# Sparse attention, then a Sinkhorn-gated mixture of experts: sums of x moved to other passes, stores and Sinkhorn rounds reordered

## The chip, the cores and the metric

The kernel runs on one core of a Trainium2 chip. The metric is the device time of one launch in microseconds, as a median of several runs. Lower is better.

## The reference

Attention with two sparse masks (a local band for half of the heads, a stride of 32 for the others), whose output is the input `x` of a mixture of eight experts. All experts run on all 2,304 tokens, and a softmax-like gate, made doubly stochastic by eight Sinkhorn rounds, weighs their outputs.

```python
scores = scale * np.matmul(q, k.transpose(0, 1, 3, 2))      # B, H, S, D = 4, 8, 576, 64
scores = np.where(masks[None, :, :, :], scores, -1000000000.0)
attn = softmax(scores)
x = (attn @ v).transpose(0, 2, 1, 3).reshape(2304, 512)

logits = x @ w_gate                                          # 512 x 8
P = np.exp(logits - logits.max())
for _ in range(8):
    P /= P.sum(1, keepdims=True) + 1e-09
    P /= P.sum(0, keepdims=True) + 1e-09
    P *= N / E
for e in range(E):                                           # 8 experts, 512 -> 1024 -> 512
    out += P[:, e:e + 1] * (np.maximum(x @ w1[e], 0.0) @ w2[e])
```

## The kernel before

Every float32 matrix product is made of three products of split operands (a high part and the rest). A split is one ScalarE copy (the high part) and one subtraction on GpSimd or VectorE (the rest).

**First stage, 36 slots.** Of 32 attention steps, eight run ahead of the loop over `slots` and one in each of its first 24 slots. A slot also takes 256 tokens through 128 hidden columns of expert 0, of whose columns the slots do the first half: `layer1` (twelve matmuls into a PSUM bank `ph`, then `rectify`, which writes `h` with ScalarE and VectorE) and `layer2` of the slot before (six matmuls into `y`). Attention writes `x`, split, into the on-chip tensor `reg`, in chunks of 512 tokens; `store_x` copies each finished chunk to memory (`xd`). At the end of a slot the list `work` runs what was put there by `at(slot, ...)`: pieces of the gate's generator `gating`, preparation of the next experts' first weights (`prep_w1`), and loads. `gating` yields 20 times: two for each of five stretches of tokens (logits, transposes), two for the start of the softmax, and one for each Sinkhorn round. A round is a chain on VectorE (sums of rows, a reciprocal, a multiplication, sums of columns), closed by one pair of matmuls `pc` that adds over partitions.

**Second stage, 90 steps `g`, three passes of 30.** A pass takes 768 tokens through all remaining 30 groups of 256 hidden columns. The first layer is a Strassen product: seven products `mul(...)` of six matmuls, on sums of weights and on sums of x (`s1` to `s4`), into the banks `ba`, `bb`, `bc`; `plus` adds them up on VectorE. In pass 1 the second layer is plain (`second`, 36 matmuls of 512 columns into `yg`, added to `acc` with the gate's weight on VectorE), and the weights' sums are formed, split and stored to memory as well (`prep_w1`, `prep_w2`). In passes 2 and 3 these are loaded again, and the second layer is a Strassen product too (`second_strassen`, 42 matmuls); there GpSimd makes most of the forms (`form_lo`, the sums in `finish_first`).

**Sums of x.** `build_s` makes `s1` to `s4` for one pass in units of 128 tokens and half of the inner columns: sums on GpSimd, a split, two stores to `sd`. For pass 1 (`p` = 0) it reads `reg`, in slots 8 to 22. For passes 2 and 3 the generator `later_sums` reads `x` back from `xd` with four loads for each unit; `next(later)` runs at the end of each step of pass 1 from `g` = 3 on, two for each of twelve units. There the rest of the split is GpSimd's.

**Order.** Instructions are issued in the order of the program, on each engine its own (the scheduling is manual), and almost all transfers are issued by SyncE, one queue: an issue that waits holds up all later ones. So the place of each call in the loops is the schedule.

Lines that matter: `store_x` L149; loads of q, k, v L202 and L204; `pc` L385; `y` stores L464; `build_s` L530, L539, L547, L550 (ScalarE copy), L553 (rest), L555 (stores); `load_w1g` L589; `prep_w1` L611 to L629 with `split` L177 and L178; `w2_sums` L643 to L650; `prep_w2` L674 to L682; matmuls of the first layer L692, of the second L721 (plain) and L822; `plus` L745; `relu_hi` and `relu_lo` L753 and L757; `m1` L914; the first scaling of `acc` by the gate L1111.

Of the kernel before, what the change touches and what calls it, by code (L numbers as in the profile page):

```python
# [55 lines left out]
def kernel(  # L56
# [9 lines left out]
    nc = tc.nc  # L66
# [358 lines left out]

    def layer1(u, c, ft):
        taken = begun[u, c[0], ft][1] if (u, c[0], ft) in begun else ()
        begin_layer1(u, c, ft, [dt for dt in range(NDT) if dt not in taken])
        rectify(u, c, ft)

    def rectify(u, c, ft):
        c0, n = c
        ph = begun.pop((u, c0, ft))[0]
        h = pools["h"].tile([P, 2, 4 * P], F32R, tag="h", name=f"h_{u}_{c0}_{ft}")
        nc.scalar.activation(h[:, 0, :n], ph[:, :n], AF.Relu)
        nc.vector.scalar_tensor_tensor(
            h[:, 1, :n], ph[:, :n], 0.0, h[:, 0, :n].bitcast(F32), op0=ALU.max, op1=ALU.subtract
        )
        hs[u, c0, ft] = h

    def layer2(u, c, ft, only=None):
# [8 lines left out]
        for i in range(nt) if only is None else only:  # L450
            y = ys[u, c0][i]
            for a, b, first in ((0, 0, True), (0, 1, False), (1, 0, False)):
                nc.tensor.matmul(  # L453
                    y, h[:, a, i * P : (i + 1) * P], w[:, b, :],
                    start=(ft == 0 and first), stop=(ft == FH - 1 and a == 1),
                )
            if ft == FH - 1:
                t = c0 // P + i
                if t < HEAD:
                    nc.scalar.activation(acc[:, t, :], y, AF.Copy)  # L460
                else:
                    o = acc[:, HEAD + t % STAGE, :]
                    nc.scalar.activation(o, y, AF.Copy)
                    nc.sync.dma_start(yd[:, t - HEAD, :], o)  # L464

# [53 lines left out]

    def build_s(p, k, th):  # L520

        st = pools["sb"].tile([P, 4, 2, P], F32, tag="sx", name=f"sx_{p}_{k}_{th}")
        x, s = st[:, :, 0, :], st[:, :, 1, :]
        t0 = 2 * TN * p + P * th
        if p:
            for i, (dh, t) in enumerate(((0, t0), (0, t0 + TN), (1, t0 + TN), (1, t0))):
                nc.sync.dma_start(st[:, i], xd[:, :, k + 2 * dh, t : t + P])  # L527
# [5 lines left out]
        else:  # L533
            for o, t in ((x[:, 0:4:3], t0), (x[:, 1:3], t0 + TN)):
                ci, c = divmod(t, CH)
                hi, lo = (
                    chunk(ci)[:, i, k : k + 3 : 2, c : c + P].bitcast(F32) for i in range(2)
                )
                nc.gpsimd.tensor_tensor(o, hi, lo, op=ALU.add)  # L539
        x11, x21, x22, x12 = (x[:, i, :] for i in range(4))  # L540
# [7 lines left out]
        yield  # L548
        so = pools["sb"].tile([P, 2, 4, P], F32R, tag="so", name=f"so_{p}_{k}_{th}")
        nc.scalar.activation(so[:, 0], s, AF.Copy)  # L550
        yield
        engine = nc.gpsimd if p else nc.vector
        engine.tensor_tensor(so[:, 1], s, so[:, 0].bitcast(F32), op=ALU.subtract)  # L553
        for j in range(2):
            nc.sync.dma_start(  # L555
                sd[:, p, :, j, k, P * th : P * (th + 1)], so[:, j].bitcast(F32)
            )
        yield
# [327 lines left out]
    def step(g):  # L886
# [16 lines left out]
        if new:  # L903
# [8 lines left out]
            part[g] = m1, u2, u3, bb, bc  # L912
            mul(g, "w11", "x11", ba, True)
            nc.scalar.activation(m1, ba[:, :TN], AF.Copy)  # L914
        if s:
# [6 lines left out]
        if new:  # L922
# [12 lines left out]
            if g >= NK:  # L935
                mul(g, "t3", "s3", bb, False)
                plus(u3, bb, m1)
                plus(u3, bc, u3)
            mul(g, "w21", "x12", ba, False)
            if strassen(g):  # L940
                r11 = r11s[g] = pools["early"].tile([P, TN], F32, tag="r11", name=f"r11_{g}")
# [8 lines left out]
            if not g:  # L950
                next(w2n, None)
                next(w2n, None)
                for x, only in rest:
                    layer2(*x, only)
            if g < NK:
                mul(g, "t3", "s3", bb, False)
# [132 lines left out]
    gat = gating()  # L1089
    for n, (k, th) in enumerate((k, th) for k in range(2) for th in range(3)):  # L1090
        w = build_s(0, k, th)
        for i in ((8, 9, 9), (10, 11, 11), (12, 15, 15), (16, 17, 17), (18, 19, 19), (19, 22, 22))[n]:
            at(i, next, w, None)
    w1_first = [prep_w1(g) for g in range(2)]
    for g, i, pieces_at in ((0, 9, (23, 24, 25, 26)), (1, 27, (29, 30, 31, 32))):
        at(i, load_w1g, g)
        for n in pieces_at:
            at(n, next, w1_first[g], None)
    for i, name in (
        (23, "x11"), (24, "s2"), (25, "s1"), (32, "x12"), (32, "s3"), (33, "x22"), (35, "s4"),  # L1100
    ):
        at(i, load_x, 0, name)
    at(27, load_w1g, 2)
    at(33, load_w2g, 0)
    for i, n in ((27, 1), (28, 2), (29, 1), (30, 1), (31, 1), (32, 1), (33, 1), (34, 1), (35, 1)):
        for _ in range(n):
            at(i, next, gat, None)
    ahead_of_second = {28: 2, 29: 1, 35: 1}

# [5 lines left out]
    slots = [(0, (c, 2 * P), ft) for c in range(0, NT, 2 * P) for ft in range(FH)]  # L1115
    prev = None
    for slot, (u, c, ft) in enumerate(slots):
# [4 lines left out]
        else:  # L1122
            layer1(u, c, ft)
        for _ in range(ahead_of_second.get(slot, 0)):
            next(gat, None)
        if slot == 1:
# [23 lines left out]
        for x in work.get(slot, ()):  # L1150
            x()
        prev = (u, c, ft)

    for x in w1_first:
        for _ in x:
            pass
    stacks["left"].close()
    stacks["sums"].close()
# [3 lines left out]
    pools["u"] = ctx.enter_context(tc.tile_pool(name="u", bufs=2, side="left"))  # L1162
    open_pools("left", ("rab", 1), ("sb", 1))

    def later_sums():
        for p in range(1, NPASS):
            for k in range(2):
                for th in range(3):
                    w = build_s(p, k, th)
                    next(w)  # L1170
                    yield
                    next(w)
                    yield
                    for _ in w:
                        pass

    later = later_sums()
    for g in range(NG + 1):
        if g == NK:
            open_pools("left", ("early", 2))  # L1180
        if g == NK + 1:
# [20 lines left out]
        p, n = divmod(g, NK)  # L1202
        if 0 < p < NPASS:
# [86 lines left out]
```

## Time and profile before

| | |
|---|---|
| median of three runs | 1582.55 us (1581.46 to 3079.31) |
| the profiled execution: its time, its span | 1586.01 us, 1584.2 us |
| busy: TensorE, its weight loads, VectorE, ScalarE, GpSimd | 98%, 92%, 83%, 35%, 66% of the span |
| moved by DMA | 433.63 MB, mean 274 GB/s |

The profile is of one execution. A row of the timeline is one instruction, or several alike in a row: start and duration in us from the start of the span, engine, line, what is written and read, its shape, how many, and in brackets how long the engine had been idle and what ended that. PE is TensorE, DVE VectorE, ACT ScalarE, POOL GpSimd, SPq the queue of SyncE. Matmuls overlap by some tenths of a microsecond, so that six in a row that start 1.04 us after the six before them may be shown with 1.20 us.

### The profile page before, as it was taken

What the parts mean: (1) busy time and instruction counts of PE and PEld (TensorE: products, weight loads), DVE (VectorE), ACT (ScalarE), POOL (GpSimd) and SP (SyncE); (2) the same over time, 40 slices, a digit from 0 to 9 for tenths busy, and PEclk for the clock granted to TensorE, in tenths of its full rate; (3) what the DMA queues carried; (4) which work ended last, traced back from release to release, by engine and by line L of the source; (5) the groups of instructions that cost most, each with busy time, mean ns of one, the idle gap of its engine ahead of it and who ended that gap; (6) DMA issues with size and microseconds to landing.
All of it is one profiled execution on the core that took longest, in us unless ns stands there. A gap on an engine that the chain in (4) does not pass through costs nothing.

```text
span 1584.2 us, 25846 instructions
## 1 busy us (share of the span) xinstructions
PE 1551.0 (98%) x9182; PEld 1459.8 (92%) x9182; DVE 1315.3 (83%) x2545; ACT 548.3 (35%) x1293; POOL 1050.0 (66%) x1033
## 2 busy tenths in 40 slices
PE   8999989999999999999999999999999999999999
PEld 6878879988888888899999999999999999999998
DVE  5656579999999999977888888888868888888887
ACT  6656234334434443333233222222143222222221
POOL 4335425776767667627787777778677778777774
PEclk9999999999999999999999999999999999999999
DMA  7466868898999989888676667667667667666662
GB/s 222 154 207 212 291 231 323 329 356 324 331 340 347 353 325 324 332 289 327 276 292 252 246 266 277 246 242 289 243 249 291 266 241 288 257 236 271 271 239 95
DMA packets 138225, 433.63 MB, mean 274 GB/s; under 512 B 10129, under 2 KB 82673, under 8 KB 123121
## 3 DMA queue, kind: packets, MB, share of 16 engines
q1 hardware_dynamic: 137952, 431.86, 72.0%
q8 instruction: 73, 1.20, 0.3%
q14 instruction: 56, 0.45, 0.1%
q10 hardware_dynamic: 144, 0.13, 0.0%
HBM read 287.20 MB, written 144.75 MB: 273 GB/s over the span
## 4 chain that ended last, share of the span: by engine, by line
PE 69%; DVE 12%; DMA 5%; POOL 5%; issue 3%; ACT 3%; SPq 3%; POOLq 0%; ACTq 0%; DVEq 0%
PE p L822 26%; PE bb L692 13%; PE ba L692 8%; PE bc L692 8%; PE yg L721 4%; DMA raws<-in_w 3%; DVE acc L728 3%; PE y L453 2%; PE ph L420 2%; POOL reg L178 2%; DVE u L745 2%; DVE w2t L682 2%; DVE w2b L682 2%; SPq L527 2%; DVE h L757 1%
## 5 line engine op out<-in xcount | busy, mean ns | idle before, releaser
L830 DVE TENSOR_TENSOR total<-p,total 128x384 f32<-128x384 f32 x770 | 400.7, 557 | 0.8 <-PE p L822 0.8
L692 PE MATMUL bb<-reg 128*128 128x384 f32 x1620 | 330.1, 338 | 10.6 <-DVE u L745 10.6
L692 PEld LDWEIGHTS bb<-reg 128*128 128x128 f32 x1620 | 285.2, 188 | 20.4 <-DVE u L745 17.9
L692 PE MATMUL ba<-reg 128*128 128x384 f32 x1080 | 217.6, 336 | 2.5 <-ACT m L914 2.2
L692 PE MATMUL bc<-reg 128*128 128x384 f32 x1080 | 217.2, 335 | 0.0
L803 ACT ACTIVATE a<-u 128x384 fp32r<-128x384 f32 x114 | 59.9, 525 | 387.5 <-DVE u L797 387.2
L692 PEld LDWEIGHTS ba<-reg 128*128 128x128 f32 x1080 | 190.5, 189 | 3.1 <-ACT m L914 2.5
L879 POOL TENSOR_TENSOR s1t<-m,u 128x384 f32<-128x384 f32 x57 | 57.9, 1016 | 202.0 <-DVE m L797 202.0
L692 PEld LDWEIGHTS bc<-reg 128*128 128x128 f32 x1080 | 189.4, 188 | 2.2 <-ACT h L753 2.2
L745 DVE TENSOR_TENSOR u<-bb,m 128x384 f32<-128x384 f32 x180 | 99.7, 554 | 110.4 <-PE bb L692 110.2
L728 DVE SCALAR_TENSOR_TENSOR acc<-yg,gate,acc 128x512 f32<-128x512 f32 x198 | 139.8, 742 | 9.7 <-PE yg L721 9.6
L721 PE MATMUL yg<-w2b,h 128*128 128x512 f32 x540 | 126.3, 392 | 0.0
L721 PE MATMUL yg<-w2t,h 128*128 128x512 f32 x540 | 125.5, 390 | 0.0
L822 PE MATMUL p<-s,w2b 128*128 128x384 f32 x696 | 125.3, 334 | 0.0
L721 PEld LDWEIGHTS yg<-w2b,h 128*128 128x128 f32 x540 | 101.9, 189 | 20.8
L822 PEld LDWEIGHTS p<-s,w2b 128*128 128x128 f32 x696 | 121.1, 188 | 0.0
L822 PE MATMUL p<-s,w2t 128*128 128x384 f32 x672 | 121.0, 334 | 0.0
L721 PEld LDWEIGHTS yg<-w2t,h 128*128 128x128 f32 x540 | 101.2, 188 | 20.5
L807 POOL TENSOR_TENSOR a<-u,a 128x384 fp32r<-128x384 f32 x114 | 117.2, 1028 | 0.0
L822 PEld LDWEIGHTS p<-s,w2t 128*128 128x128 f32 x672 | 116.9, 188 | 0.0
L745 DVE TENSOR_TENSOR u<-bc,u 128x384 f32<-128x384 f32 x180 | 99.6, 553 | 4.1 <-PE bc L692 1.0
L178 POOL TENSOR_TENSOR reg<-rt,reg 128x512 fp32r<-128x512 f32 x28 | 36.3, 1297 | 94.1 <-ACT reg L177 94.1
(147 smaller groups left out, 2862.3 us busy)
## 6 DMA issues: line engine op xcount, KB each, us to landing
reg<-wd SPq DMA_DIRECT2D x56, 1792.0 KB
wd<-reg SPq DMA_DIRECT2D x30, 1792.0 KB
w2b<-w2d SPq DMA_DIRECT2D x27, 1792.0 KB
w2t<-w2d SPq DMA_DIRECT2D x26, 1792.0 KB
w2d<-w2b SPq DMA_DIRECT2D x15, 2048.0 KB
w2d<-w2t SPq DMA_DIRECT2D x15, 2048.0 KB
raws<-in_w SPq DMA_DIRECT2D x68, 256.0 KB
sd<-so SPq DMA_DIRECT2D x36, 256.0 KB
```

Source lines behind the costliest of these rows:

```text
L178: nc.gpsimd.tensor_tensor(lo, src, hi.bitcast(F32), op=ALU.subtract)
L420: nc.tensor.matmul(ph[:, :n], w[:, i, dt, :], xv(x, dt, c0, n), start=(first and len(taken) == 1 and i + x == 0), stop=(len(taken) == NDT ...
L682: nc.vector.tensor_tensor(w[:, 1, : 4 * Q], src, w[:, 0, : 4 * Q].bitcast(F32), op=ALU.subtract)
L692: nc.tensor.matmul(out[:, :TN], w[:, i, k, :], xops[x][:, xi, k, :], start=(start and n == 0), stop=(n == 5), skip_group_check=True,)
L721: nc.tensor.matmul(y, hg[g, i // 3, f][:, a, o : o + P], w[:, b, f, :], start=(f == 0 and a + b == 0), stop=(f == 1 and a == 1),)
L728: nc.vector.scalar_tensor_tensor(acc[:, i, :], y, gate[:, t, e : e + 1], acc[:, i, :], op0=ALU.mult, op1=ALU.add)
L745: nc.vector.tensor_tensor(o, bank[:, :TN], s, op=ALU.add)
L803: nc.scalar.activation(t[:, 0], src, AF.Copy)
L807: nc.gpsimd.tensor_tensor(t[:, 1], src, t[:, 0].bitcast(F32), op=ALU.subtract)
L822: nc.tensor.matmul(y[:, :TN], w[:, b, wi, d, :], h[:, a, :], start=(a + b == 0), stop=(a == 1),)
L830: nc.vector.tensor_tensor(o, y[:, :TN], o, op=ALU.add)
L879: nc.gpsimd.tensor_tensor(s1, m1, u3, op=ALU.add)
```

## The change

- `build_s` takes a width and whether it reads `reg` (`direct`). The six units of pass 2 are built, as those of pass 1, from `reg` in the slots (12 units, first stage in slots 8 to 25). The units of pass 3 stay with `later_sums`, in halves of 64 tokens (12 units), and `next(later)` runs in steps 32 to 59, which is pass 2.
- Of a unit in the slots, the split's two halves run together one slot after the sums, and the two stores to `sd` one slot later still. Rows of `y` go through `outbox` and are stored at the end of the slot after the one that made them.
- `layer1` can run rounds of `gating` between its matmuls and `rectify`. They run there in slots 27 to 35; the last two come in step 0, after its first product and after its fourth.
- The first scaling of `acc` runs on GpSimd as six multiplications with a broadcast operand, in step 0 behind the rest of `layer2`; before, ScalarE ran it at the end of step 0.
- `prep_w1(0)` moves from slots 23 to 26 to slots 23, 26, 27, 28; the raw weights of `g` = 1 are loaded in slot 28 and not 27; `x11`, `s2`, `s1` are loaded in slots 28, 28, 29 and not 23, 24, 25.

```diff
-    def layer1(u, c, ft):
+    def layer1(u, c, ft, between=0):
         taken = begun[u, c[0], ft][1] if (u, c[0], ft) in begun else ()
         begin_layer1(u, c, ft, [dt for dt in range(NDT) if dt not in taken])
+        for _ in range(between):
+            next(gat)
         rectify(u, c, ft)
...
                     nc.scalar.activation(o, y, AF.Copy)
-                    nc.sync.dma_start(yd[:, t - HEAD, :], o)
+                    outbox.append((yd[:, t - HEAD, :], o))
...
-    def build_s(p, k, th):
+    def build_s(p, k, o, w, direct):
-        st = pools["sb"].tile([P, 4, 2, P], F32, tag="sx", name=f"sx_{p}_{k}_{th}")
+        st = pools["sb"].tile([P, 4, 2, w], F32, tag="sx", name=f"sx_{p}_{k}_{o}")
...
-        so = pools["sb"].tile([P, 2, 4, P], F32R, tag="so", name=f"so_{p}_{k}_{th}")
+        so = pools["sb"].tile([P, 2, 4, w], F32R, tag="so", name=f"so_{p}_{k}_{o}")
         nc.scalar.activation(so[:, 0], s, AF.Copy)
+        engine = nc.vector if direct else nc.gpsimd
+        engine.tensor_tensor(so[:, 1], s, so[:, 0].bitcast(F32), op=ALU.subtract)
         yield
-        engine = nc.gpsimd if p else nc.vector
-        engine.tensor_tensor(so[:, 1], s, so[:, 0].bitcast(F32), op=ALU.subtract)
         for j in range(2):
-            nc.sync.dma_start(
-                sd[:, p, :, j, k, P * th : P * (th + 1)], so[:, j].bitcast(F32)
-            )
+            nc.sync.dma_start(sd[:, p, :, j, k, o : o + w], so[:, j].bitcast(F32))
...
             mul(g, "w11", "x11", ba, True)
+            if not g:
+                next(gat)
             nc.scalar.activation(m1, ba[:, :TN], AF.Copy)
...
             mul(g, "w21", "x12", ba, False)
+            if not g:
+                assert next(gat, gat) is gat
...
                 for x, only in rest:
                     layer2(*x, only)
+                send_out()
+                for i in range(HEAD):
+                    nc.gpsimd.tensor_tensor(
+                        acc[:, i, :], acc[:, i, :], gate[:, i, 0:1].to_broadcast([P, D]),
+                        op=ALU.mult,
+                    )
...
-    for n, (k, th) in enumerate((k, th) for k in range(2) for th in range(3)):
-        w = build_s(0, k, th)
-        for i in ((8, 9, 9), (10, 11, 11), (12, 15, 15), (16, 17, 17), (18, 19, 19), (19, 22, 22))[n]:
-            at(i, next, w, None)
+    units = [(p, k, P * th) for p in range(2) for k in range(2) for th in range(3)]
+    for x, i in zip(units, (8, 9, 11, 12, 14, 15, 19, 20, 21, 22, 24, 25)):
+        w = build_s(*x, P, True)
+        for n in range(3):
+            at(i + n, next, w, None)
     w1_first = [prep_w1(g) for g in range(2)]
-    for g, i, pieces_at in ((0, 9, (23, 24, 25, 26)), (1, 27, (29, 30, 31, 32))):
+    for g, i, pieces_at in ((0, 9, (23, 26, 27, 28)), (1, 28, (29, 30, 31, 32))):
...
-        (23, "x11"), (24, "s2"), (25, "s1"), (32, "x12"), (32, "s3"), (33, "x22"), (35, "s4"),
+        (28, "x11"), (28, "s2"), (29, "s1"), (32, "x12"), (32, "s3"), (33, "x22"), (35, "s4"),
...
-    for i, n in ((27, 1), (28, 2), (29, 1), (30, 1), (31, 1), (32, 1), (33, 1), (34, 1), (35, 1)):
-        for _ in range(n):
-            at(i, next, gat, None)
-    ahead_of_second = {28: 2, 29: 1, 35: 1}
+    for i in (27, 27, 28):
+        at(i, next, gat, None)
+    ahead_of_second = {27: 1, 28: 1, 29: 2, **{i: 1 for i in range(30, 36)}}
...
+        send, keep = keep, []
+        for x in send:
+            nc.sync.dma_start(*x)
+        keep, outbox[:] = outbox[:], []
...
     def later_sums():
-        for p in range(1, NPASS):
-            for k in range(2):
-                for th in range(3):
-                    w = build_s(p, k, th)
+        for k in range(2):
+            for o in range(0, TN, P // 2):
+                w = build_s(2, k, o, P // 2, False)
...
-            if g == 0:
-                assert next(gat, gat) is gat
-                for i in range(HEAD):
-                    scale(0, i)
-            if g > 2:
-                next(later, None)
         elif g < NK + KEEP:
             for store in put_off[g - NK :: KEEP]:
                 store()
+        elif g < 2 * NK:
+            next(later, None)
```

## Rows read from the trace of the kernel before

**Rows 1.** Who waited for whom, TensorE, whole span: us, times, longest

```profile
PE bb L692 <- DVE u L745: 10.6, 23, 0.9
PE pc L385 <- DVE g L382: 6.2, 5, 2.5
PE ba L692 <- ACT m L914: 2.2, 1, 2.2
```

**Rows 2.** Windows, one step each: length, busy (instructions) by engine, PE clock, DMA share, GB/s

```profile
256.72:272.23 15.51, 15.51 (x80) 14.07 (x80) 15.21 (x21) 6.26 (x11) 8.98 (x8) 1.00 0.87 316
...
303.47:319.80 16.33, 16.01 (x79) 14.00 (x79) 15.15 (x20) 6.28 (x12) 12.66 (x14) 1.00 0.95 344
...
662.60:678.11 15.51, 15.51 (x80) 14.07 (x80) 13.83 (x21) 6.11 (x11) 4.90 (x4) 1.00 0.77 288
```

**Rows 3.** Timeline of VectorE, the same line without and with sums of x alongside

```profile
268.75 0.55 DVE L757 SCALAR_TENSOR_TENSOR h<-u,h 128x384 fp32r<-128x384 f32 x1
...
431.31 1.08 DVE L757 SCALAR_TENSOR_TENSOR h<-u,h 128x384 fp32r<-128x384 f32 x1
```

**Rows 4.** Timelines of SyncE's queue and of TensorE, 78 to 100 us

```profile
78.58 1.43 SPq L555 DMA_DIRECT2D sd<-so  x2
...
83.46 0.53 SPq L149 DMA_DIRECT2D xd<-reg  x1
84.09 0.96 SPq L202 DMA_DIRECT2D qk<-in_qkv  x1
...
95.36 0.56 PE L220 MATMUL sc<-qk 64*64 64x96 f32 x16 [1.77 <-DMA qk<-in_qkv]
...
97.67 3.23 PE L348 MATMUL pl<-reg,wgs 128*128 128x512 f32 x8
```

**Rows 5.** Window over the last rounds and steps 0 and 1, columns as Rows 2

```profile
181.00:226.00 45.00, 35.41 (x189) 31.58 (x188) 31.85 (x82) 17.07 (x32) 13.63 (x12) 0.93 0.58 212
```

**Rows 6.** Timeline of TensorE: the last rounds before step 0, and step 1

```profile
199.72 0.39 PE L385 MATMUL pc<-g,ones 128*128 128x8 f32 x2 [0.94 <-DVE g L382]
202.57 0.47 PE L385 MATMUL pc<-g,ones 128*128 128x8 f32 x2 [2.47 <-DVE g L382]
...
221.91 1.32 PE L692 MATMUL ba<-reg 128*128 128x384 f32 x6 [2.18 <-ACT m L914]
```

**Rows 7.** Timelines of ScalarE and GpSimd around the first scaling

```profile
216.88 3.79 ACT L1111 ACTIVATE acc<-acc,gate 128x512 f32<-128x512 f32 x6 [1.28 <-DVE gate L389]
...
222.46 1.30 POOL L178 TENSOR_TENSOR reg<-ra,reg 128x512 fp32r<-128x512 f32 x1 [29.33 <-ACT reg L177]
```

**Rows 8.** Groups of GpSimd's instructions by shape: count, busy us, mean ns, idle before

```profile
L547 POOL TENSOR_TENSOR sx<-sx 128x128 f32<-128x128 f32 x72 | 31.7, 462 | 2.8
...
L530 POOL TENSOR_TENSOR sx<-sx 128x256 f32<-128x256 f32 x24 | 21.6, 919 | 0.0
...
L539 POOL TENSOR_TENSOR sx<-reg 128x256 f32<-128x256 f32 x12 | 8.5, 731 | 0.0
```

**Rows 9.** Timeline of TensorE, layer2 of slots 3, 4 and 11, 12

```profile
43.73 1.66 PE L453 MATMUL y<-w2t,h 128*128 128x512 f32 x6
48.52 1.68 PE L453 MATMUL y<-w2t,h 128*128 128x512 f32 x6
...
84.68 1.66 PE L453 MATMUL y<-w2t,h 128*128 128x512 f32 x6
89.47 1.68 PE L453 MATMUL y<-w2t,h 128*128 128x512 f32 x6
```

**Rows 10.** Timeline of SyncE's queue, and a window, columns as Rows 2

```profile
180.74 8.76 SPq L464 DMA_DIRECT2D yd<-acc  x4
...
185.00:190.00 5.00, 3.72 (x23) 3.13 (x24) 4.27 (x11) 2.87 (x7) 3.87 (x4) 1.00 0.13 52
```

**Rows 11.** A step of pass 2: window, columns as Rows 2; timeline of GpSimd

```profile
940.00:954.57 14.57, 14.57 (x86) 14.57 (x85) 12.53 (x24) 3.84 (x8) 11.04 (x11) 1.00 0.64 253
...
966.79 1.02 POOL L879 TENSOR_TENSOR s1t<-m,u 128x384 f32<-128x384 f32 x1 [3.36 <-DVE m L797]
```

More of the change, by code (lines that the diff above doesn't have):

```diff
@@ L439, in rectify @@
         hs[u, c0, ft] = h
+    outbox = []
     def layer2(u, c, ft, only=None):
@@ L518 @@
     wraw, w2raw, w2s, hg, yg, part = {}, {}, {}, {}, {}, {}
-    def build_s(p, k, th):
-        st = pools["sb"].tile([P, 4, 2, P], F32, tag="sx", name=f"sx_{p}_{k}_{th}")
+    def build_s(p, k, o, w, direct):
+        st = pools["sb"].tile([P, 4, 2, w], F32, tag="sx", name=f"sx_{p}_{k}_{o}")
         x, s = st[:, :, 0, :], st[:, :, 1, :]
-        t0 = 2 * TN * p + P * th
-        if p:
+        t0 = 2 * TN * p + o
+        if direct:
+            for d, t in ((x[:, 0:4:3], t0), (x[:, 1:3], t0 + TN)):
+                ci, c = divmod(t, CH)
+                hi, lo = (
+                    chunk(ci)[:, i, k : k + 3 : 2, c : c + w].bitcast(F32) for i in range(2)
+                )
+                nc.gpsimd.tensor_tensor(d, hi, lo, op=ALU.add)
+        else:
             for i, (dh, t) in enumerate(((0, t0), (0, t0 + TN), (1, t0 + TN), (1, t0))):
-                nc.sync.dma_start(st[:, i], xd[:, :, k + 2 * dh, t : t + P])
+                nc.sync.dma_start(st[:, i], xd[:, :, k + 2 * dh, t : t + w])
             yield
@@ L532, in build_s @@
                 )
[L533 to L537, printed above, removed]
-                )
-                nc.gpsimd.tensor_tensor(o, hi, lo, op=ALU.add)
         x11, x21, x22, x12 = (x[:, i, :] for i in range(4))
@@ L548, in build_s @@
         yield
-        so = pools["sb"].tile([P, 2, 4, P], F32R, tag="so", name=f"so_{p}_{k}_{th}")
+        so = pools["sb"].tile([P, 2, 4, w], F32R, tag="so", name=f"so_{p}_{k}_{o}")
         nc.scalar.activation(so[:, 0], s, AF.Copy)
+        engine = nc.vector if direct else nc.gpsimd
+        engine.tensor_tensor(so[:, 1], s, so[:, 0].bitcast(F32), op=ALU.subtract)
         yield
-        engine = nc.gpsimd if p else nc.vector
-        engine.tensor_tensor(so[:, 1], s, so[:, 0].bitcast(F32), op=ALU.subtract)
         for j in range(2):
-            nc.sync.dma_start(
-                sd[:, p, :, j, k, P * th : P * (th + 1)], so[:, j].bitcast(F32)
-            )
+            nc.sync.dma_start(sd[:, p, :, j, k, o : o + w], so[:, j].bitcast(F32))
         yield
@@ L954, in step @@
                     layer2(*x, only)
+                send_out()
[3 more added lines that the diff above has]
+                        op=ALU.mult,
+                    )
             if g < NK:
@@ L1115 @@
     slots = [(0, (c, 2 * P), ft) for c in range(0, NT, 2 * P) for ft in range(FH)]
-    prev = None
+    prev, keep = None, []
     for slot, (u, c, ft) in enumerate(slots):
@@ L1122 @@
         else:
-            layer1(u, c, ft)
-        for _ in range(ahead_of_second.get(slot, 0)):
-            next(gat, None)
+            layer1(u, c, ft, ahead_of_second.get(slot, 0))
         if slot == 1:
@@ L1156, with send_out @@
             pass
+    def send_out():
+        for x in keep + outbox:
+            nc.sync.dma_start(*x)
     stacks["left"].close()
@@ L1162 @@
     pools["u"] = ctx.enter_context(tc.tile_pool(name="u", bufs=2, side="left"))
-    open_pools("left", ("rab", 1), ("sb", 1))
+    open_pools("left", ("rab", 1))
     def later_sums():
-        for p in range(1, NPASS):
-            for k in range(2):
-                for th in range(3):
-                    w = build_s(p, k, th)
[L1170 to L1175, printed above, removed]
+        for k in range(2):
+            for o in range(0, TN, P // 2):
+                w = build_s(2, k, o, P // 2, False)
+                next(w)
+                yield
+                next(w)
+                yield
+                for _ in w:
+                    pass
     later = later_sums()
@@ L1179 @@
         if g == NK:
-            open_pools("left", ("early", 2))
+            open_pools("left", ("early", 2), ("sb", 1))
         if g == NK + 1:
```

## Prediction

> **What bounds the kernel now.** I read the waits first. TensorE waits in three places that this change touches: for `plus` ahead of the last product of pass 1's steps, 10.6 us in 23 times; for Sinkhorn rounds, 6.2 us; once 2.2 us for ScalarE [rows 1]. Then the windows, one step each, because a mean over the span hides the stages. A step of pass 1 without sums of x lasts 15.51 us with TensorE busy all of it, one with them 16.33 [rows 2]. Of passes 2 and 3 a step is 14.57 us, TensorE without a gap [rows 11]: nothing is to be won there. Last the timelines of the two places before pass 1 where TensorE stood still: one late load of q and k at 95 us [rows 4], and the stretch 181 to 226 us, in which it was busy 35.4 of 45.0 us at a mean granted clock of 0.93, that is, partly at 1.2 in place of 2.4 GHz [rows 5].
>
> **Sums leave pass 1.** The reader is to see that the long steps have no more matmuls, but up to 12.7 us of GpSimd in place of 9.0, with VectorE at 15.2 of 15.5 already without them [rows 2]. The one slows the other: a subtraction that took 0.55 us takes 1.08 beside the sums [rows 3]. So `plus` comes late and TensorE waits. The long steps run from 303.47 to 662.60 us, 22 of them of 16.32 us; the two before them (272.23 to 303.47) are 0.1 longer each than 15.51 [rows 2]. 22 x 0.81 + 0.2 = 18.1 us. All of it goes if every step is like 256.72 to 272.23. But there VectorE has only 0.3 us of room, so TensorE may lose half of that 0.1 in each of the 24 steps, 1.2 in all. I take 17.5; bounds 16.3 and 18.1.
>
> **Sums for pass 2 in the slots.** A unit costs GpSimd two sums of 0.73 us and four of 0.46, 3.3 us [rows 8], as well as a copy and a subtraction. TensorE covers it: from slot 11 to slot 12, with a unit's sums at work, its `layer2` matmuls start 4.79 us apart, and 4.79 from slot 3 to slot 4, without one [rows 9]. GpSimd also has each slot's normalizing, so four units in a row fill it; what waits for that is the transposes one slot later. I take nothing. Without the cover, half of each sum of the six new units would show, 10 us; below nothing there is nothing to win, as these slots have no wait of this kind.
>
> **Stores a slot later.** At 78.58 us SyncE's queue stands before a unit's stores, which wait for the split; behind them are the store of a chunk of x (83.46) and the load of q and k (84.09) that TensorE waits 1.77 us for at 95.36 [rows 4]. Issued a slot later, these stores hold up nothing there, and chunk and load go out earlier; no row says by how much, and I take it to be more than the 1.77. The wait is followed by a lower clock: eight logits matmuls take 3.23 us [rows 4]. For that I take half of the loss over 181 to 226 us, where two waits over 2 us did the same: 0.07 x 45.0 = 3.15 us [rows 5], so 1.6. Together 3.4; bounds 0 (the chunk of x still lies ahead of the load) and 3.4.
>
> **Rounds and scaling, 181 to 226 us.** 9.6 us idle and 3.15 of clock, 12.7 in all [rows 5]. Term by term:
> - A round with nothing beside it makes TensorE wait 2.47 us [rows 6]; that was the seventh, at the end of slot 35. It now comes behind the first product of step 0 (84 matmuls are a step of 14.57 us [rows 11], so its six take 1.04), and 1.4 remain. The other waits for rounds, 6.2 - 2.47 = 3.7 us, come in three slots where GpSimd slows the chain, and once, 0.94, in slot 35 [rows 6]. The order within a slot changes nothing for the three, as a round still needs the round before; the fourth goes. So -1.1 and -0.9.
> - The last round moves ahead of VectorE's work on the second weights, and GpSimd's six scalings begin right then. A GpSimd operation of this size takes 1.30 us [rows 7], so 7.8 us in which four operations of VectorE, ahead of the `plus` that TensorE waits for (0.9 at 213.64, the longest of its kind [rows 1]), can be stretched by 0.53 each [rows 3]. Bounds: 0 and +2.1; the late chain adds to that, so I take +0.8.
> - ScalarE no longer holds 3.79 us of scaling ahead of the copy of `ba`: the 2.18 us wait goes [rows 6, 7], and 0.3 beside it. GpSimd has been idle for 29 us by then [rows 7], so its scalings delay nothing of its own. -2.5.
> - One of the two clock drops goes with the 2.18, -1.6; bounds 0 and -3.15.
>
> Sum -5.3; bounds -1 and -12.7.
>
> The Trainium skill, page "SBUF — State Buffer", section "Who interferes with whom", has GpSimd and a VectorE operation with two SBUF inputs exclude each other for a whole instruction. Here a stretch of 0.53 us stands beside GpSimd operations of 1.30, so less than a whole one [rows 3, 7]. By the rule the four operations could lose 1.30 each, an estimate of 5.2 in place of 0.8, and the sum below would be 4.4 us smaller.
>
> **Loads before step 0.** `x11`, `s2`, `s1` move from slots 23 to 25 into a busy stretch, and the raw weights of `g` = 1 now go behind the store of `g` = 0's. But between 185 and 190 us DMA is used at 0.13, as the queue stands 8.76 us before stores of `y`, which are put off now [rows 10]. That room takes most of it. I allow 1.0 us for late raw weights; bounds 0 and 4.
>
> **Sums for pass 3 in pass 2.** GpSimd is idle for 3.36 us of each step, just where `next(later)` puts the work [rows 11]. A half unit's sums: two of half of 0.92, four of 0.23 to 0.46 [rows 8], so 1.8 to 2.8 us every second step; the other steps get a subtraction and a copy. All within 3.36; DMA is at 0.64. I take nothing. Upper bound: 0.5 us in each of 24 steps, 12 us, if the first form of the next step comes that late and all slack is gone.
>
> **Sum.** -17.5 - 3.4 - 5.3 + 1.0 = -25.2. The profiled execution, 1586.0, would be 1560.8. It lies 3.5 over the median of the runs shown, so the median goes from 1582.55 to 1557.4 us, 1.6% faster.
>
> **Rivals.**
> 1. Everything before pass 1 goes right: 18.1 + 3.4 + 12.7 = 34.2 us, so 1548. For it: each of the waits has a part of the change aimed at it. Against it: rounds are a chain, and moving them ahead of `rectify` doesn't shorten it. Faster than 2% needs 31.7, so 10.2 of the 12.7.
> 2. VectorE becomes the bound of pass 1. It is busy 15.21 of 15.51 us without the sums [rows 2], and its operations change with how they meet GpSimd's. With one more of them stretched, 15.21 + 0.53 = 15.74 us, and 24 x 0.23 = 5.5 of the full 18.1 is lost, 4.9 of my 17.5: 1562.3. Against it: two steps without sums, one early and one late, run at 15.51 [rows 2].
> 3. The slots pay: six units at 1.0 us, and 4 for late loads in place of 1.0, so 9 less: 1566.5. For it: four units in a row fill GpSimd, and ScalarE and VectorE stand in order behind it. Against it: slots 11 and 12 [rows 9].
> 4. The load of q and k stays late: 1561; within the forecast's own range.
> 5. Slower than before: pass 2. If GpSimd's additions don't fit into its gap, its 11 us chain of forms [rows 11] starts late and the second layer's matmuls wait for it. The kernel is slower than before once that costs 25.2 / 24 = 1.05 us a step, and slower by 2% from (25.2 + 31.7) / 24 = 2.4 us. At 1.5 us: 1593. Against it: 2.8 is under 3.36 even at the dear end.
>
> **Chances.** About 2%, 31.7 us, is what a measurement of this kernel can tell from no change. The forecast with rival 4, from 1552 to 1561.5: 0.64. Rival 1: 0.11, nearly all of it under the 2% line. Rival 2: 0.11. Rival 3: 0.10. Rival 5: 0.04, of which 0.02 would be over 2% slower. Range 1548 to 1566: it takes in rivals 1 and 2 and most of 3. Faster 0.10, same 0.88, slower 0.02.
>
> **What would show it.** Right: step 256 to 272's length in all steps of pass 1 and no waits `bb` for `plus`; no wait for q and k after the warm-up; nothing over 2 us before `ba` in step 1, with one wait of some 1.4 before `pc` in step 0; 14.57 us steps in pass 2 with GpSimd's idle time ahead of the first form down to some 1 us. Wrong: a wait of transposes for GpSimd's normalizing in slots 20 to 26; ScalarE idle for raw weights for more than 3 us around slot 29; waits of TensorE for forms in pass 2, which would make even the sign doubtful.

## The result and the profile after

| | before | after |
|---|---|---|
| median of the runs, us | 1582.57 | 1568.91 |
| profiled execution, us | 1586.01 | 1568.56 |
| its span, us | 1584.2 | 1566.7 |

The ratio is 0.9917, 95% interval 0.9904 to 0.9931: 13.7 us gained, under 1%, where 25.2 were forecast. The time lies 2.9 us above the upper end of the range.

In the trace after, code lines are 2 to 4 higher: 694 for 692 (products), 747 for 745 (`plus`), 682 and 684 for 680 and 682 (second weights). First who waited for whom, TensorE, whole span (us in total, times, longest), the answer to [rows 1]:

```profile
PE y L457 <- ACT h L437: 6.0, 1, 6.0
PE bb L694 <- DVE u L747: 5.4, 1, 5.4
...
PE pc L385 <- DVE g L382: 1.3, 1, 1.3
```

The 23 waits for `plus` have become one. The five for rounds have become one, and the one for ScalarE is gone. In their place stand two long waits, one in the last slots and one between steps 0 and 1, before pass 1 runs evenly. The windows (length, busy and instructions by engine, clock, DMA share, GB/s) show two steps of pass 1, the answer to [rows 2], one step of pass 2, the answer to [rows 11], and the two stretches with the long waits:

```profile
256.87:272.37 15.50, 15.50 (x80) 14.06 (x79) 14.99 (x21) 6.27 (x11) 8.96 (x8) 1.00 0.87 320
303.51:319.01 15.50, 15.50 (x80) 14.06 (x79) 15.16 (x21) 6.27 (x11) 10.38 (x9) 1.00 0.97 360
...
184.00:190.00 6.00, 4.29 (x14) 3.74 (x15) 3.34 (x10) 2.32 (x5) 4.51 (x5) 0.50 1.01 360
216.00:222.00 6.00, 5.96 (x21) 5.96 (x22) 3.27 (x6) 3.24 (x7) 2.12 (x3) 0.57 0.62 184
...
720.37:734.94 14.57, 14.57 (x85) 14.57 (x85) 12.43 (x24) 3.88 (x9) 13.52 (x18) 1.00 0.68 268
```

Pass 1 did what was forecast: 15.50 us a step with TensorE busy all of it. In pass 2 the step is 14.57 us as before, with GpSimd now at 13.5 us of it. Each long wait is followed by TensorE at its lower level, 1.2 GHz (granted clock 0.50 and 0.57). Where the first one comes from, in the timelines of SyncE's queue, ScalarE and TensorE:

```profile
176.41 4.39 SPq L591 DMA_DIRECT2D raws<-in_w  x4
...
184.75 0.63 ACT L177 ACTIVATE reg<-raws 128x512 fp32r<-128x512 f32 x1 [10.01 <-DMA raws<-in_w]
...
185.71 2.93 PE L457 MATMUL y<-w2t,h 128*128 128x512 f32 x6 [6.02 <-ACT h L437]
```

The raw weights of `g` = 1 are asked for at 176.41 us and land at 184.75. ScalarE stands 10 us before the first piece of `prep_w1(1)`, and the rectifying that TensorE needs is queued behind it. What stands ahead of this load in SyncE's queue after, and then the load and its first use before:

```profile
165.21 7.97 SPq L559 DMA_DIRECT2D sd<-so  x4
173.28 1.46 SPq L591 DMA_DIRECT2D ra<-in_w  x2
...
169.05 5.94 SPq L589 DMA_DIRECT2D raws<-in_w  x4
...
181.11 0.63 ACT L177 ACTIVATE reg<-raws 128x512 fp32r<-128x512 f32 x1 [2.57 <-DMA raws<-in_w]
```

`layer2` of slot 28 begins at 173.61 us before and at 170.51 after. Counted from there the load is asked for 10.5 us later and used 6.7 us later, where a slot is about 3 us. The stores of the last two units' sums hold the queue for 7.97 us, and the loads for `g` = 2 (`ra`, `rb`), which came behind it before, now go ahead of it. The second long wait, in the timelines of GpSimd, ScalarE, VectorE and TensorE:

```profile
207.60 7.64 POOL L963 TENSOR_TENSOR acc<-acc,gate 128x512 f32<-128x512 f32 x6 [13.33 <-DMA raws<-in_w]
...
208.77 1.06 ACT L682 ACTIVATE w2b<-raws 128x1024 fp32r<-128x1024 f32 x1 [1.63 <-DMA raws<-in_w]
...
209.92 1.80 DVE L684 TENSOR_TENSOR w2b<-raws,w2b 128x1024 fp32r<-128x1024 f32 x1 [1.93 <-DMA yd<-acc]
211.64 1.52 DVE L645 TENSOR_TENSOR w2sum<-raws 128x512 f32<-128x512 f32 x1
213.19 1.15 DVE L648 TENSOR_TENSOR w2sum<-raws,w2sum 128x256 f32<-128x256 f32 x1
214.37 1.14 DVE L649 TENSOR_TENSOR w2sum<-w2sum,raws 128x256 f32<-128x256 f32 x1
...
216.04 2.29 PE L694 MATMUL bb<-reg 128*128 128x384 f32 x6 [5.38 <-DVE u L747]
```

ScalarE gets the second weights 1.63 us late, and then four operations of VectorE run beside the six scalings. TensorE waits 5.38 us for the `plus` behind them, where before it waited 0.9 [rows 1].

### The profile page after: what moved, and what is told of

The parts are those of the page before. It is cut to its first block, busy times and chain, and to the rows that moved or that the text cites. A ratio compares the mean times of both kernels' runs of the same rounds, so it can differ in the third digit from the quotient of the medians.

```text
span 1566.7 us, 25951 instructions
## 1 busy us (share of the span) xinstructions
PE 1541.5 (98%) x9182; PEld 1460.8 (93%) x9182; DVE 1316.5 (84%) x2551; ACT 544.7 (35%) x1293; POOL 1060.1 (68%) x1075
## 4 chain that ended last, share of the span: by engine, by line
PE 96%; DMA 2%; DVE 1%; SPq 1%; POOL 0%; issue 0%; ACT 0%; POOLq 0%
PE p L824 27%; PE bb L694 18%; PE yg L723 17%; PE bc L694 12%; PE ba L694 12%; PE y L457 3%; PE ph L420 3%; PE tp L285 1%; PE sc L237 1%; DMA qk<-in_qkv 1%; DMA yd<-acc 1%; PE pv L298 1%; PE pv L312 1%; PE pl L348 1%; PE sc L220 1%; DMA raws<-in_w 0%
## 5 line engine op out<-in xcount | busy, mean ns | idle before, releaser
L881 POOL TENSOR_TENSOR s1t<-m,u 128x384 f32<-128x384 f32 x57 | 57.9, 1016 | 163.1 <-DVE m L799 163.1
L178 POOL TENSOR_TENSOR reg<-ra,reg 128x512 fp32r<-128x512 f32 x28 | 48.1, 1718 | 89.6 <-ACT reg L177 89.6
```

The costliest lines, as they stand in the source:

```text
L178: nc.gpsimd.tensor_tensor(lo, src, hi.bitcast(F32), op=ALU.subtract)
L881: nc.gpsimd.tensor_tensor(s1, m1, u3, op=ALU.add)
```

## The experiments

Theory A: the 11.5 us that are missing are two late things before step 1, each with its own price: the raw weights, asked for too late, and the scalings on GpSimd. Rivals: the price is one that both share (the lower clock); part of the gain was never there (the late load of `q` and `k`); sums left pass 1 at no cost only by chance.

### Pieces of group 1 later

```diff
-    for g, i, pieces_at in (..., (1, 28, (29, 30, 31, 32))):
+    for g, i, pieces_at in (..., (1, 28, (33, 34, 35, 35))):
```

> The changed kernel with one edit: the four pieces of the second group's first weights (prep_w1(1)) run at the end of slots 33, 34, 35, 35 and no longer 29 to 32; their load stays where it is. Theory (ScalarE stands in order behind the raw weights, which land at 184.75 us, and with it the rectified h that TensorE's layer2 needs): the 6.0 us wait of TensorE in slot 31 and the 3.4 us lost to its lower clock afterwards go, slots 29 to 33 are about 3.1 us each. The pieces free the raw buffers later against the rest, so the second weights of g = 0 land later against step 0, and part comes back there as a longer wait for VectorE's plus ahead of step 1: 4 to 8 us faster than the changed kernel in all, 1561 to 1565. Rival (GpSimd's backlog from four units in a row, or the rounds ahead of rectifying, hold up h): the wait stays near 6 us and the time near 1569.

Measured: 1565.6 us, ratio 0.9893 (0.9879 to 0.9906). This kernel overwrites part of what it still needs: the load of `g` = 0's second weights in slot 33 stands ahead of pieces that read the same buffer, so part of group 1's first weights is replaced by others. The waits of TensorE:

```profile
PE bb L694 <- DVE h L438: 5.6, 1, 5.6
...
PE bb L694 <- DVE u L747: 3.4, 1, 3.4
```

The wait of 6.0 is gone from slot 31, but ScalarE waits in the last slots instead. As the weights that it waits for are the ones loaded in between, the run shows that ScalarE's place in the queue decides, and not more.

### Raw weights asked for a slot earlier

```diff
-    (8, 9, 11, 12, 14, 15, 19, 20, 21, 22, 24, 25)
+    (8, 9, 11, 12, 14, 15, 19, 20, 21, 22, 26, 27)
-    ((0, 9, (23, 26, 27, 28)), (1, 28, (29, 30, 31, 32)))
+    ((0, 9, (23, 24, 25, 26)), (1, 27, (30, 31, 32, 33)))
```

> The changed kernel with the raw weights ahead of the last two units: prep_w1(0) in slots 23 to 26 and the load of g = 1's raw weights in slot 27 (both as in the kernel before), pieces of prep_w1(1) in slots 30 to 33, and the last two units of pass 2 start in slots 26 and 27 in place of 24 and 25. Theory (late raw weights): they land some 4 us earlier, near 181, ScalarE asks for them one slot later, so TensorE's wait in slot 31 falls from 6.0 to under 1 us and the clock stays up there: 8 to 10 us faster than the changed kernel, 1559 to 1561, as the buffers come free early too. Rival (backlog of GpSimd): no unit less is built, so the wait moves by no more than the order and 1567 to 1569 remain.

The edit does more than its slot: the load now stands ahead of the loads for `g` = 2 and of the stores of the last two units, which come two slots later.

Measured: 1564.6 us, ratio 0.9885 (0.9869 to 0.9900), 4.3 less than after. The wait of 6.0 us is gone. Short ones are back: for rounds 2.4 us in three waits in place of 1.3 in one, and 1.4 ahead of `pm`, the transpose at the start of the softmax. The other long one grew from 5.4 to 6.6 us, as the second weights come later still (ScalarE's timeline):

```profile
205.35 1.06 ACT L682 ACTIVATE w2b<-raws 128x1024 fp32r<-128x1024 f32 x1 [3.08 <-DMA raws<-in_w]
```

So the late raw weights are worth 4.3 us here, less than expected: the rounds had hidden behind that wait, and the second weights take part of it back.

### First scaling on ScalarE, ahead of the sums of the second weights

```diff
             next(w2n, None)
             if not g:
+                for i in range(HEAD):
+                    scale(0, i)
                 next(w2n, None)
                 next(w2n, None)
...
-                for i in range(HEAD):
-                    nc.gpsimd.tensor_tensor(
-                        acc[:, i, :], acc[:, i, :], gate[:, i, 0:1].to_broadcast([P, D]),
-                        op=ALU.mult,
-                    )
```

> The changed kernel with the six first scalings on ScalarE, in step 0 behind the copy of the first second-layer weights, where ScalarE stands idle for 5.7 us; nothing else changes. Theory (GpSimd's scalings and VectorE's operations with two operands from SBUF slow each other): the four VectorE operations ahead of plus take 1.22, 0.69, 0.42, 0.43 us again in place of 1.80, 1.52, 1.15, 1.14, the wait of TensorE ahead of step 1 falls from 5.4 to about 2.5 us, and with a shorter wait the lower clock lasts less: 3 to 6 us faster, 1563 to 1566. Rival (the wait is for the second weights, which land late): 1.6 of the 5.4 us are that; if they were all of it the time stays at 1569.

Measured: 1564.3 us, ratio 0.9883 (0.9869 to 0.9896), 4.6 less than after. The same four operations of VectorE with GpSimd idle, and the scalings on ScalarE:

```profile
211.07 1.23 DVE L684 TENSOR_TENSOR w2b<-raws,w2b 128x1024 fp32r<-128x1024 f32 x1 [0.19 <-ACT w2b L682]
212.21 0.69 DVE L645 TENSOR_TENSOR w2sum<-raws 128x512 f32<-128x512 f32 x1
212.93 0.42 DVE L648 TENSOR_TENSOR w2sum<-raws,w2sum 128x256 f32<-128x256 f32 x1
213.39 0.43 DVE L649 TENSOR_TENSOR w2sum<-w2sum,raws 128x256 f32<-128x256 f32 x1
...
210.88 3.77 ACT L1120 ACTIVATE acc<-acc,gate 128x512 f32<-128x512 f32 x6
```

They take 2.77 us in place of 5.61: 2.84 us are the stretch, 0.57 to 0.83 each. The wait falls to 0.8 us, by more than this, because the 1.63 us of late second weights don't show here: TensorE begins the fourth product of step 0 at 208.16 us and not at 205.41 (a round makes it wait 0.8 us more, and the granted clock is 0.72 over 204 to 210), and by then the weights are there. The 3.77 us on ScalarE cost nothing in this place; what cost 2.2 us in the kernel before was where they stood, ahead of the copy of `ba` [rows 6, 7].

### Second weights asked for earlier, nothing else

```diff
-    at(33, load_w2g, 0)
+    at(31, load_w2g, 0)
```

> The kernel after with one edit: the second weights of group 0 are asked for in slot 31 in place of 33. Theory (of the 5.38 us that TensorE waits for u at 216.0, 1.63 are ScalarE's wait for these weights, 2.85 the VectorE operations stretched beside the scalings): the wait falls to 3.5 to 4.0, VectorE's L684, L645, L648, L649 stay at 1.8, 1.5, 1.15, 1.14 us, the y wait of 6.0 stays; 1567 to 1568, about 1.5 less than after. Rival (the late weights push the four operations into the scalings; come in time, they are done before): the wait falls under 2 us, with the lower clock behind it gone too, 1563 to 1565.

Measured: 1566.2 us, ratio 0.9900 (0.9885 to 0.9914), 2.7 less than after. Timelines of VectorE and TensorE:

```profile
208.13 1.54 DVE L684 TENSOR_TENSOR w2b<-raws,w2b 128x1024 fp32r<-128x1024 f32 x1 [0.19 <-ACT w2b L682]
209.60 1.52 DVE L645 TENSOR_TENSOR w2sum<-raws 128x512 f32<-128x512 f32 x1
...
214.00 1.52 PE L694 MATMUL bb<-reg 128*128 128x384 f32 x6 [3.39 <-DVE u L747]
```

The weights come in time, the stretch stays, and the wait is 3.39 us. Of the 5.38, 2.0 are the late weights and what moves with them; most of the rest are the scalings on GpSimd. The rival, that weights in time would be done ahead of the scalings, falls.

### Both edits

> The kernel after with both edits of the last two runs: the raw weights of group 1 are asked for in slot 27 (first pieces of group 0 at 23 to 26, of group 1 at 30 to 33, last two units of sums at 26 and 27), and the six first scalings stand on ScalarE in step 0. Theory (two misses, each with its own price): the gains add, 4.3 and 4.6 us against 1568.9, so 1559 to 1561, with neither the 6.0 us wait at 185.7 nor the 5.4 us wait at 216. Rival A (the two misses share one price, the lower clock that follows the first idle stretch): 1563 to 1565. Rival B (the second weights of group 0 land late and take the place of the scalings): the wait of bb at 216 stays at 3 us or more, 1562 to 1565.

Measured: 1561.5 us, ratio 0.9873 (0.9858 to 0.9888), 7.4 less than after; the single gains make 8.9. The profiled execution, 1564.5, is the slowest of the four, 3.0 above the median, so its waits need not be those of the others. Waits of TensorE, and ScalarE's timeline:

```profile
PE bb L694 <- DVE u L747: 4.0, 1, 4.0
PE pc L385 <- DVE g L382: 3.0, 4, 1.3
...
PE pm L369 <- DVE gb L366: 1.4, 1, 1.4
```

```profile
206.45 1.06 ACT L682 ACTIVATE w2b<-raws 128x1024 fp32r<-128x1024 f32 x1 [3.08 <-DMA reg<-sd]
```

The prices nearly add, so the first rival (one shared price) falls. Rival B is there too: the late second weights take the place of the scalings. They are asked for at 192.31 us, behind a store of 1.8 MB of first weights, while the DMA engines are fully used:

```profile
190.00:206.00 16.00, 13.96 (x81) 12.43 (x80) 12.03 (x38) 1.91 (x5) 3.99 (x5) 1.00 1.04 415
```

### Both edits and the second weights ahead of that store

```diff
-    at(33, load_w2g, 0)
+    at(32, load_w2g, 0)
```

> As the kernel with both edits, and the second weights of group 0 are asked for in slot 32 instead of 33, ahead of the fourth piece and of the store of the first weights that its queue holds until that piece is done. If the second weights land late there: 1.5 to 3 us less than the kernel with both edits, and no DMA wait of ScalarE's L682. Rival (the scalings alone made that stretch late): the same time within 0.5 us.

Measured: 1557.3 us, ratio 0.9847 (0.9833 to 0.9862): 11.6 us less than after and the fastest of all. The waits for rounds and ahead of `pm` are as with both edits; of the long one this is left:

```profile
PE bb L694 <- DVE u L747: 0.8, 1, 0.8
```

The third edit moves one place in a list and is worth 4.3 us, by the medians and by the profiled executions (1564.5 and 1560.2). That is more than the expected 1.5 to 3, and the waits alone don't make it: `bb` waits 3.2 us less. TensorE's timelines show the rest. With both edits its wait is followed by a granted clock of 0.50 over 210 to 216 us, and from that wait's end to `second` it takes 9.95 us, here 7.49. Against it stands 1.6 us for a stretch at 0.72 (198 to 204) that the execution profiled here has and the other has not; this execution, too, is 2.9 us above its median.

### Rounds behind rectifying again

```diff
-        for _ in range(between):
-            next(gat)
         rectify(u, c, ft)
+        for _ in range(between):
+            next(gat)
```

> As the kernel with both edits, and in slots 27 to 35 the Sinkhorn rounds stand behind the rectifying of the slot again. Theory of the prediction (the order is worth about 1 us, VectorE's rounds end earlier in the slot): 0.5 to 2 us slower than the kernel with both edits, with pc waits of 2 to 6 us in total in slots 28 to 35. Rival (rounds are hidden either way): same within 0.5 us. Rival (rounds ahead delay h, and with it the y of the next slot): 1 to 3 us faster.

> The kernel with both edits and the early second weights (1557.3), and in slots 27 to 35 the Sinkhorn rounds stand behind the rectifying again. With no late weights to blur it: theory of the prediction, the order is worth about 1 to 2 us (the pc waits were 4.9 us in total with the rounds behind, 3.0 with the rounds ahead), so 1558.3 to 1559.3. Rival (the chain of rounds ends at the same time, and what is lost in the slots comes back in step 0): 1557 within 0.5.

On top of both edits: 1560.0 us, some 1.5 *less* than with the rounds ahead, though the rounds make TensorE wait more. The executions overlap (1559.7 to 1562.1 against 1560.5 to 1564.5), so this sign is not clear of their spread. On top of the fastest kernel: 1560.4 (ratio 0.9860, 0.9844 to 0.9877), 3.1 *more*. The waits, first kernel, then second:

```profile
PE pc L385 <- DVE g L382: 4.9, 4, 1.9
...
PE bb L694 <- DVE u L747: 1.3, 1, 1.3
```

```profile
PE pc L385 <- DVE g L382: 4.5, 4, 1.9
...
PE bb L694 <- DVE u L747: 0.8, 1, 0.8
```

The waits for rounds grow by 1.9 and by 1.5 us. In the first kernel the second weights were there earlier, at 205.2 us on ScalarE in place of 206.5, and the wait for `bb` is 1.3 us in place of 4.0, which pays for that and more in the profiled executions; why they were there earlier is not shown. Where these weights are in time, the order shows its own worth. The other 1.6 of the 3.1 us I can't place: both profiled executions have one stretch at a lower clock, 0.72 over 6 us, and they differ by 0.5 us only (1560.2 and 1560.7). The other three of the fastest kernel took 1557.1 to 1557.4; whether they go without that stretch no run shows.

### Stores a slot later, alone, in the kernel before

```diff
-                    nc.sync.dma_start(yd[:, t - HEAD, :], o)
+                    outbox.append((yd[:, t - HEAD, :], o))
...
+        send, keep = keep, []
+        for x in send:
+            nc.sync.dma_start(*x)
+        keep, outbox[:] = outbox[:], []
```

and the stores to `sd` of a unit a slot after its split.

> The kernel before with one part of the change: the rest of the split right behind the copy and the stores of sums a slot later, and the rows of y stored at the end of the slot after the one that made them. Theory (prediction): the load of q and k leaves earlier, the 1.77 us wait at 95 us and the lower clock after it go, 3.4 us: 1579. Rival (the wait is in the profiled execution, which took 1586.0, but not in most runs, whose median is 1582.6): the profile shows no wait, and the median stays within 1 us of the kernel before.

Measured: 1583.5 us, ratio 1.0006 (0.9997 to 1.0015). No gain, and TensorE doesn't wait for `q` and `k` after the warm-up. That left open whether the kernel before waits there as a rule.

### The kernel before, profiled again

> The kernel before, unchanged, profiled once more. If the load of q and k that was late at 95 us in its first profiled execution (1586.0) is the rule: a wait of 1.7 us or more at 95 us again, lower clock behind it, and a time near 1586. If it is that one execution's own: no such wait, and 1582 to 1583, as the median of its runs; then the 3.4 us of the prediction's sum were never in the median to be won.

1583.4 us. Its waits of TensorE:

```profile
PE bb L692 <- DVE u L745: 10.5, 23, 0.9
PE pc L385 <- DVE g L382: 6.7, 5, 2.5
...
PE ba L692 <- ACT m L914: 2.2, 1, 2.2
```

All as in [rows 1], but the 1.77 us at 95 us [rows 4] aren't there, nor the lower clock behind them. From `layer2` of slot 1 to that of slot 28 the first profile took 141.5 us, this one 138.1. So the 3.4 us were rightly sized, but they belong to that one execution and not to the median.

### Sums for pass 3 back in pass 1, half and full width

```diff
             if g == 4:
                 gate_rows()
+            if g > 2:
+                next(later, None)
...
-        elif g < 2 * NK:
-            next(later, None)
```

and for full width units of 128 tokens in place of 64.

> The kernel after with the sums for pass 3 back in pass 1 (half a unit wide as there, one stage of a unit in each of some 25 steps) instead of in pass 2. Theory (a GpSimd sum beside u = u2 + m1 on VectorE stretches it, and TensorE waits for u): the sums are half as long as those of the kernel before, so about 0.3 to 0.5 us in each of some 25 steps, 8 to 12 us slower than the kernel after, 1577 to 1581, with bb waits on u in the steps that have sums. Rival (it was the number of operations in flight, not their length, that counted): 0.8 us a step as before, 1586 to 1590. Rival (half-wide sums slip beside the short operations): same within 2 us.

> The kernel after with the sums for pass 3 in pass 1 as in the run with half units, but in full units, 128 columns wide as in the kernel before: 6 units, two steps each. Theory (VectorE has about 0.3 us of room in a step; only full-wide sums stretch its operations by more than that): the 12 steps that have a unit take 16.3 in place of 15.5 us, 8 to 11 us slower than the kernel after, 1577 to 1580. Narrower form of it (only the step with the sums themselves, not the one with the split): 6 x 0.81 = 5 us, 1573 to 1575. Rival (it was never the width; something else that moved with the change freed the steps): the same as after, 1567 to 1571.

Half width: 1568.5 us, ratio 0.9913 (0.9898 to 0.9928), the same as after. Full width: 1577.7, ratio 0.9969 (0.9958 to 0.9980), 8.8 more than after. One step of each with some of its VectorE operations, and the GpSimd operation that begins the next weights' sums (L619), half width first:

```profile
303.51:319.01 15.50, 15.50 (x79) 14.06 (x79) 15.00 (x21) 6.45 (x11) 11.62 (x14) 1.00 0.94 342
```

```profile
310.66 0.57 DVE L649 TENSOR_TENSOR w2sum<-w2sum,raws 128x256 f32<-128x256 f32 x1
...
312.87 1.29 POOL L619 TENSOR_TENSOR rt<-rb,ra 128x512 f32<-128x512 f32 x1
...
314.49 0.91 DVE L759 SCALAR_TENSOR_TENSOR h<-m,h 128x384 fp32r<-128x384 f32 x1
315.32 1.09 DVE L759 SCALAR_TENSOR_TENSOR h<-u,h 128x384 fp32r<-128x384 f32 x1
```

```profile
303.74:320.05 16.31, 15.96 (x80) 13.98 (x79) 15.12 (x20) 6.28 (x12) 12.64 (x14) 1.00 0.97 348
```

```profile
312.31 0.84 DVE L649 TENSOR_TENSOR w2sum<-w2sum,raws 128x256 f32<-128x256 f32 x1
...
315.64 1.29 POOL L619 TENSOR_TENSOR rt<-rb,ra 128x512 f32<-128x512 f32 x1
...
316.19 1.16 DVE L759 SCALAR_TENSOR_TENSOR h<-m,h 128x384 fp32r<-128x384 f32 x1
317.27 1.09 DVE L759 SCALAR_TENSOR_TENSOR h<-u,h 128x384 fp32r<-128x384 f32 x1
```

Full sums bring the step of 16.3 us back, 11 times, 9.1 us in all. In the step with half sums the same operations are stretched, two of them by 0.5 us less together, and it costs nothing: in these two runs the price is not in proportion to the length but begins at a point. What runs beside the two subtractions L759 are not the sums of x themselves but the weights' sums behind them, which in the kernel after begin at 309.02 us in this step, with half sums at 312.87 and with full ones at 315.64. I had expected 8 to 12 us from the half ones.

## Why the prediction was wrong

The terms of its sum, against the trace of the kernel before profiled again (without the late load) and the one after. The starts of slots and steps are read from TensorE's timeline.

| term | forecast, us | measured, us | from |
|---|---|---|---|
| pass 1 | -17.5 | -18.2 | second layer of step 2 to that of step 31: 468.03 to 449.85 |
| stores later, load of `q`, `k` | -3.4 | 0 | ratio 1.0006; no such wait in the second profile |
| rounds, scaling, loads before step 0 | -5.3 + 1.0 | +2.7 | slot 28 to step 2: 68.03 to 70.76 |
| sums in the slots | 0 | +0.6 | slot 1 to 28: 138.1 to 138.7 |
| passes 2, 3 and the end | 0 | +0.5 | from step 31 on: 875.1 to 875.6 |
| sum | -25.2 | -14.4 | spans 1581.6 to 1566.7: -14.9, of which 0.5 lie ahead of slot 1 |

The starts, before and after: `layer2` of slot 1 at 32.30 and 31.79 us, of slot 28 at 170.42 and 170.51; second layer of step 2 at 238.45 and 241.27, of step 31 at 706.48 and 691.12. By the medians it is 13.7.

**Pass 1** was right, in mechanism and size: no wait for `plus`, every step as long as 256.72 to 272.23 had been, and VectorE didn't become the bound (rival 2). One reading behind it was not exact. Beside the subtraction of 1.08 us at 431.31 [rows 3] GpSimd doesn't work on sums of x but on the weights' sums, which the sums of x had pushed there:

```profile
431.06 0.93 POOL L620 TENSOR_TENSOR ru<-ra,rt 128x256 f32<-128x256 f32 x1
432.06 0.92 POOL L621 TENSOR_TENSOR ru<-rb,ru 128x256 f32<-128x256 f32 x1
```

What the two runs with the sums put back add is that the sums for pass 3 need not have left pass 1: at half width they cost nothing there. Whether those for pass 2 would fit in beside them was not run.

**Stores a slot later** was wrong as a term. The wait had one row, of one execution that was 3.5 us above the median. I took it out of the profiled execution and then lowered the result by those 3.5 us as well. The second profile shows that the late load was most of the difference (1586.0 and 1583.4), so the same microseconds were counted twice. For the median the term is nothing.

**Loads before step 0** is the step that failed first. I wrote of the room that the stores of `y` had left, "That room takes most of it", and took 1.0 us. But that room is at 180.74 us and later [rows 10], and the raw weights are asked for at 176.41: ahead of it. The kernel before already waited 2.57 us for this load, at 181.11 us on ScalarE. And the load did not move by one slot: I named the store of `g` = 0's weights as what it goes behind, and that took 0.4 us (175.97); I left out the stores of the last two units' sums and the loads for `g` = 2, and with them it was used 6.7 us later. The wait was 10.0 us on ScalarE and 6.0 on TensorE, above my bound of 4, with the lower clock behind it. So the sums in the slots, which I priced at nothing, cost TensorE little in the slots themselves (0.6 us) but delayed the queue. The run with the load a slot earlier and ahead of all this prices it at 4.3 us, net of the waits for rounds that it hid. My own list named the sign, ScalarE idle for raw weights around slot 29.

**Scalings on GpSimd**, "I take +0.8", was mis-sized: 2.84 us, above my bound of 2.1. I used 0.53 us, the stretch of another operation, for one and a half of four; all four were hit, by 0.57 to 0.83 us each. The rule of the Trainium skill ("SBUF — State Buffer", section "Who interferes with whom") gave 5.2 as an estimate. The trace lies between the two: the operations that by the rule meet do meet, all four, yet each loses a half to two thirds of a GpSimd operation of 1.27 us (7.64 / 6) and not all of it. What I had not priced at all is the 1.63 us of late second weights on ScalarE. Together they are the growth from 0.9 to 5.38: 2.84 + 1.63 = 4.47.

**One clock drop less** fell with these two. There are still two stretches at 1.2 GHz, now with 0.50 and 0.57 as the mean over 6 us; the second profile of before has two as well, and 0.72 in each.

**Rounds ahead.** Of the waits forecast, 1.4 us ahead of `pc` in step 0 came (1.32) and the `ba` wait of 2.2 went. That the order within a slot changes nothing for the other three was wrong in both directions: in the kernel after they are hidden by the 6.0 us wait, and without that wait the order saves 1.5 us of waiting in all (4.5 and 3.0), 0.9 of it in the slots.

**Rivals.** The third (the slots pay, loads late) came nearest in time, 1566.5, with its mechanism half right: loads cost more than the 4 us that it gave them, the slots themselves 0.6 and not 6, though their stores are part of why the load came late. The fifth didn't come: GpSimd's additions fit into pass 2, the idle time ahead of its first form falling from 202.0 to 163.1 us in total.

The fastest kernel of the experiments, 1557.3, stands at the forecast's number, but it does not make the forecast right. Its 25.2 us are made otherwise, without the 3.4 and without the scalings on GpSimd.

## What to carry to other kernels

A load that is moved later is priced at its landing: from the row of the first instruction that waits for it, plus the move, plus what the same change puts ahead of it in the queue that issues it, and with what stands behind it on the engine that waits. Room that a change opens in a queue helps only what is asked for after it. A wait that one profile shows is checked against the median before it becomes a term of a sum. And work put on GpSimd beside VectorE is costed at every operation that it covers, by the nearest row of the same operation, and then compared with the slack of that stretch.

## What was not expected of the hardware

- Six GpSimd multiplications of 1.27 us each lengthened the four VectorE operations on the second weights beside them (1.23 to 1.80, 0.69 to 1.52, 0.42 to 1.15, 0.43 to 1.14 us), short ones by more than their own length, while GpSimd's stayed near the 1.30 us of a like operation [rows 7]. A `plus`, which reads one operand from PSUM, kept its 0.54 us (215.44) beside a GpSimd operation of 1.46 us.
- Full-width sums of x on GpSimd took the step from 15.51 to 16.31 us. Half-width sums left it at 15.50, although they, too, stretched the two subtractions shown, to 0.91 and 1.09 us from the 0.56 and 0.55 of the kernel after.
- With the DMA engines fully used (share 1.04 over 16 us), second weights that were asked for at 192.3 us were waited for until 206.4; asked for 2 us earlier, in another kernel and ahead of a store of 1.8 MB, they were in time for their use at 204.6.
